# Tails of weight blocks gathered in DRAM, the second MLP weight loaded a group ahead, and two gelus moved at the seam

## The chip, the cores and the metric

The kernel runs on one core of one Trainium2 chip. A core has TensorE (matmuls into PSUM), VectorE, ScalarE, GpSimd and SyncE; in the kernel's text they are `pe`, `dve`, `act`, `pool` and `sp`. DMAs are issued here from SyncE (plain copies) and from GpSimd (copies that add to what lies at the destination, `accum_op`). Each engine works through its own instructions in the order in which the program issues them. The metric is the device time of one execution in microseconds, lower is better.

## The reference

The input x has 2048 tokens of 576 channels, all in float32. With xn = layernorm(x), the output is x plus an attention block on xn plus a mixer block on xn.

```python
# A: attention, 32 heads of 18, a window of 8 keys at distances 0, 2, ... 14
qkv = xn @ wqkv;  attn = softmax(q . k[s - off] / sqrt(18))
A = (attn @ v) @ wo
# B: shift mixing, then an MLP with 4608 hidden channels
h  = gelu(layernorm(xn) @ w1);  hs = four quarters of h, shifted by +1, -1, +2, -2 tokens
x1 = xn + hs @ w2
B  = x1 + gelu(layernorm(x1) @ w3) @ w4
out = x + A + B
```

The change lies in the MLP, w3 (576 x 4608) and w4 (4608 x 576), which takes over half of the time.

## The kernel before

Each float32 operand is split into a high part (type fp32r, made by ScalarE with a cast) and a low remainder (made by VectorE with a subtract), and a product is built of high-high, high-low and low-high matmuls. The low part of a 64-row tail shares a tile with its high part.

The program runs in stages: the projection to q, k, v; the token mixing (`mix_tile`, `mix_rem`, loop over four blocks b of 512 tokens and five column tiles i); x1; and then the MLP. The hidden channels of the MLP are worked off in chunks of 256. The first four chunks (`NPL = 4`) are plain. The remaining 14 (`NWP`) are done twice, once for each half of the tokens (sb = 0, 1): 28 groups q = 0 to 27. The second half goes through the chunks backwards (`pair(q)`), so that groups 13 and 14, the seam, share their weights.

In a group, a 2 x 2 block product (two halves of the 576 rows of w3, two hidden tiles of 128, two token blocks) is made from seven products instead of eight, from sums of blocks: of the weights (`combine`, VectorE, four instructions at line 956) and of the activations (DRAM sums `td`, GpSimd's accumulating DMAs in `sums`). `product` (line 1117) issues seven matmuls for each product, in the order of `HALVES`; the last of them, (0, 0), reads the tail rows of the weight. The seven products are called P1 to P7; they are interleaved with eight down tiles, D0 to D7, which multiply the gelus of the group before with w4 (`down`, matmuls at line 862). D0 to D3 read the hidden tiles c12 and c22, D4 to D7 read c11 and c21. c12, c21 and c22 have one buffer each. A down tile is accumulated in one of two PSUM buffers, which ScalarE (lines 867, 870) or VectorE (873) evicts; `ahead` then opens the buffer for the tile after next, for some tiles with a copy of the sum so far (843).

The order of the work around this is written out by hand. `ORDER` gives the sequence of a usual group, and `plan` holds, for each item, what is issued behind it:

```python
ORDER = "P1 D0 P2 P6 D1 P5 D2 P7 D3 P4 D4 P3 D5 D6 D7"
ORDERS = {..., NWP - 1: "P1 D0 P2 P6 P5 P7 D1 P4 P3 D2 D3 D4 D5 D6 D7",
          NWP: "D0 D1 P1 D2 P2 P6 D3 P5 P7 D4 P4 P3 D5 D6 D7"}
```

The steps of a group, as far as the change touches them:

- `load_pair(q)` (lines 945 and 948, SyncE) loads the chunk's part of w3 into the one staging tile `w3st` (`WS["st", q]`): two DMAs of 256 KB and four of 64 KB, the tail rows once for each 32 partitions. It is issued for a later group at D6, when `w3st` is free.
- `split_a(n)` makes the tile `w3a` of the next group from three plain blocks of `w3st`: step 0 a cast on ScalarE (961), step 1 a signed copy of the tail rows on ScalarE (963) and an accumulating DMA from GpSimd (964) that adds the raw tail rows onto 32 partitions, so that these hold the remainder, step 2 a subtract on VectorE (967). Steps 0 and 1 are issued at D1, step 2 at D2.
- `combine(n)` overwrites the blocks in `w3st` with their sums. It is issued at P4.
- `split_s(n)` makes `w3s`, which has one buffer, from the sums in the same three steps (at P3 and D5); its accumulating DMA reads the sums in `w3st`.
- `load_w4(c)` (560, SyncE) loads 576 KB of w4 into unused parts of Y, at P1 of its own group; `split_w4(c)` casts it on ScalarE (567, at D3) and subtracts on VectorE (570, at D4).
- `gelu22` and `gelu12` (814, 815, ScalarE) write c22 and c12, `low22` and `low12` (820, VectorE) their low parts; `z_add` is line 1127, `keep` line 1123.
- At the seam, `get_op` (911, 913) loads the activations of the second half of the tokens, and `split_op` (921, 926, 927 on ScalarE, 595 on VectorE) splits them, in two parts each: B11, B21, T2, T1, T3, T4, B22.
- Attention runs in the gaps: `bg` lets a generator issue so many microseconds of VectorE work behind each item, with its loads and stores on SyncE (693, 696, 722), until a few groups before the end. In the last groups `load_o` (1165), `o_turn` and `put_o` prepare its output, and a last stage multiplies that with wo.

Of the kernel before, what the change touches and what calls it, by code (L numbers as in the profile page):

```python
# [8 lines left out]
F32 = mybir.dt.float32  # L9
F32R = mybir.dt.float32r  # L10
AF = mybir.ActivationFunctionType
ALU = mybir.AluOpType
# [4 lines left out]
S, D, F = 2048, 576, 4608  # L17
# [12 lines left out]
HF = D // 2  # L30
# [27 lines left out]
def fused_block(ctx, tc, x, wqkv, wo, w1, w2, w3, w4, out):  # L58
# [36 lines left out]
    xd = {}  # L95
    qkvd = dram.tile([24, HALO + S, GC], F32, name="qkvd")
    od = dram.tile([S, D], F32, name="od")
    yd = {t: dram.tile([128, D], F32, name=f"yd{t}") for t in YD}
    xn = [dram.tile([D, 512], F32, name=f"xn{b}") for b in range(NB)]
    td = {(sb, k): dram.tile([HF, 512], F32, name=f"td{sb}{k}")  # L100
# [405 lines left out]
    for b in range(NB):  # L506
        for i, m in enumerate((0, 1, 2, 4, 3) if b < 3 else (4, 0, 1, 2, 3)):
            if m < 4:
                mix_tile(b, m)
            else:  # L510
                todo += mix_rem(b)
            if b + 1 < NB and i in (1, 2):
                split_x(xring["z", b + 1], i - 1)
            for _ in range((0, 1, 1, (1, 2, 2, 2, 3)[i])[b]):
                todo.pop(0)()
            if b == 0 and i < 2:
                w2raw[i] = load_w2(i)
            if b + 2 < NB and i == 4:
                get(("z", b + 2), ring_block(("z", b + 2)))
            k = {(0, 4): 0, (1, 1): 1, (1, 4): 2, (2, 1): 3, (2, 4): 4}.get((b, i))  # L520
            if k is not None:
                split_w(W2[:, k, :], W2[:, 5 + k, :], w2raw[k])
                if k < 3:
                    w2raw[k + 2] = load_w2(k + 2)
# [27 lines left out]
        spent[0] += 0.82  # L552
        split_w(W3[f][:, 0:5, :], W3[f][:, 5:10, :], raws[f])

    def load_w4(c, eng=sp):
        t = W4["pair", c] = wp.tile([128, 2, 2, D], F32R, name="w4", bufs=2)
        for i in range(2):
            f = 2 * c + i
            W4[f] = t[:, i]
        eng.dma_start(Y[:, 0:4, :].rearrange("p (a b) c -> p a b c", b=2)[:, :, 1, :],  # L560
                      w4[c * 256:(c + 1) * 256, :].rearrange("(a p) d -> p a d", p=128))

    def split_w4(c, step=None):
        t = W4["pair", c]
# [372 lines left out]
    def pair(q):  # L937
        return q if q < NWP else 2 * NWP - 1 - q
# [17 lines left out]
            dve.tensor_tensor(st[:, :, o, :], st[:, :, o, :], st[:, :, i, :], op=op)  # L956


    def split_ws(dst, src, steps):
        if 0 in steps:  # L960
            act.copy(dst[:, 3:5], src[:, 1:3])  # L961
        if 1 in steps:
            act.activation(dst[0:96, 0], src[0:96, 0], AF.Identity, scale=TS)
            pool.dma_start(dst[32:64, 0].bitcast(F32), src[32:64, 0], accum_op=ALU.add)
        if 2 in steps:
            spent[0] += 1.1
            dve.tensor_tensor(dst[:, 1:3], src[:, 1:3], dst[:, 3:5].bitcast(F32), op=ALU.subtract)

    def split_a(q, steps=(0, 1, 2)):
        if 0 in steps:  # L970
            WA[q] = wp.tile([128, 15, 128], F32R, name="w3a", bufs=2).rearrange(
                "p (s o) c -> p s o c", s=5)
        split_ws(WA[q], WS["st", q][:, :, 1:4, :], steps)

    def split_s(q, steps=(0, 1, 2)):
        if 0 in steps:
            WS[q] = wspool.tile([128, 20, 128], F32R, name="w3s").rearrange(
                "p (s o) c -> p s o c", s=5)
        split_ws(WS[q], WS["st", q], steps)

    def place(k):
        return opool.tile([128, 5, 512], F32R, name=f"big{k}")
# [199 lines left out]
    for q in range(NQ):  # L1182
# [33 lines left out]
        def at(it, f, *args):  # L1216
            plan.setdefault(it, []).append(lambda: f(*args))
# [13 lines left out]
            at("P3", load_pair, q + 2)  # L1231
        elif q == NWP - 1:
            rtemps[:] = [2, 13]
            at("P1", load_w4, p)
            for it, k in zip(("P1", "P2", "P6", "P5", "P7", "P4", "P3"),
                             ("B11", "B21", "T2", "T1", "T3", "T4", "B22")):
                at(it, get_op, 1, k)
            at("P4", split_w4, p)
            at("P4", gelu22)
            at("P3", split_op, 1, "B11", 0)  # L1240
            at("P3", low22)
            at("D2", split_op, 1, "B11", 1)
            at("D2", gelu12)
            at("D3", split_op, 1, "B21", 0)
            at("D4", low12)
            at("D4", split_op, 1, "B21", 1)
            at("D5", split_op, 1, "T2", 0)
            at("D6", split_op, 1, "T2", 1)
            at("D7", split_op, 1, "T1", 0)
        elif q == NWP:  # L1250
            rtemps[:] = [2]
            at("D0", split_op, 1, "T1", 1)
            at("D1", split_op, 1, "T3", 0)
            at("P1", split_op, 1, "T3", 1)
            at("D2", split_op, 1, "T4", 0)
            at("P2", split_a, n, (0, 1))
            at("P6", split_a, n, (2,))
            at("P6", split_op, 1, "T4", 1)
# [8 lines left out]
            at("D5", split_s, n, (2,))  # L1267
            at("D6", low12)
        elif z < -1:
            at("P1", load_w4, p)  # L1270
            at("D1", split_a, n, (0, 1))
            at("D2", split_a, n, (2,))
            at("D3", split_w4, p, 0)
            at("P4", combine, n)
            at("P4", gelu22)
            at("D4", low22)
            at("D4", split_w4, p, 1)
            at("P3", split_s, n, (0, 1))
            at("D5", gelu12)
            at("D5", split_s, n, (2,))  # L1280
# [11 lines left out]
        if -5 <= z <= -2:  # L1292
            for i, (it, nx) in enumerate((("P6", "D1"), ("P7", "D3"), ("P3", "D5"), ("D6", "D7"))):
                t = 4 * (z + 5) + i
                at(it, o_turn, t)
                if t + 3 < NT:
                    at(nx, load_o, t + 3)

        if 0 < q < 9:
            at("D6", sums, 1, q - 1)  # L1300
        if 0 < q <= len(YD):
# [1 line left out]
        if -4 <= z < -1:  # L1303
            at("P1", put_o, z + 4)
        if z == -2:
            at("D7", load_w4, NPL + pair(q + 1))
            at("D7", put_o, 3)

        if z == -1:
# [147 lines left out]
```

## Time and profile before

| | |
|---|---|
| median of 3 runs | 1311.72 us (1311.17 to 1312.82) |
| the profiled execution | 1307.43 us |
| its span, first to last instruction | 1305.7 us |
| mean granted clock of TensorE | 0.990 |
| busy: TensorE matmuls, weight loads | 1263.4 us, 1158.4 us |
| busy: VectorE, ScalarE, GpSimd | 919.9, 747.8, 258.9 us |
| moved by DMA | 226.14 MB, 173 GB/s in the mean |

PE is TensorE's matmuls and PEld its weight loads, which run beside them; DVE is VectorE, ACT ScalarE, POOL GpSimd, SPq SyncE's queue of DMA issues. A row of the timeline gives the start and the duration in microseconds, the engine and line, the operation, the tiles written and read with their shapes, how many instructions were merged, and in brackets how long the engine had been idle before it and what ended that. A wait for several things is put down to the one that came last by the profile. A row of the groups gives the busy time, the mean duration in ns of one, and the idle time before them. In a row of the chain of waits there are start, duration and what ran. The last numbers of a row of a window are the granted clock, the DMA engines' busy share and GB/s; before them stand the window's length and the busy time of PE, PEld, DVE, ACT and POOL. A row of DMA issues ends with the KB of one and the median time from issue to landing in microseconds.

### The profile page before, as it was taken

To read this page: it belongs to the slowest core of one execution; us is meant where nothing else is said; L and a number is where in the kernel's file an instruction comes from. 1 tells how busy PE (TensorE), PEld (TensorE's weight loads), DVE (VectorE), ACT (ScalarE), POOL (GpSimd) and SP (SyncE) were. 2 spreads that over 40 slices of the span, in tenths; PEclk is the share of its full clock that TensorE was granted. 3 is DMA by queue.
4 is the path that set the end of the run, shared out by engine and by line. 5 is a ranking of instruction groups with operands and counts; after the bars stand their busy time and mean duration, and the time that the engine had idled before them with its cause. 6 is when DMAs were issued, how large, how long until landed. Compare 5 with 4: busy or idle time off the path is not lost.

```text
span 1305.7 us, 20016 instructions
## 1 busy us (share of the span) xinstructions
PE 1263.4 (97%) x7482; PEld 1158.4 (89%) x7482; DVE 919.9 (70%) x1226; ACT 747.8 (57%) x1188; POOL 258.9 (20%) x374
## 2 busy tenths in 40 slices
PE   9999999999999999899979999989999999999998
PEld 8999998899889998788968889978999989998898
DVE  6456535778468987579967989978999994455342
ACT  4322226536546546677656677757777767667730
POOL 2011100021221121123222232212222222222100
PEclk9999999999999999999989999989999999999999
DMA  7646874256888898479878779795876767899982
GB/s 212 154 109 149 171 159 145 69 159 181 192 214 202 194 217 193 88 180 202 192 166 169 193 135 214 165 230 123 206 163 111 184 124 147 194 217 221 252 252 82
DMA packets 204641, 226.14 MB, mean 173 GB/s; under 512 B 79856, under 2 KB 139728, under 8 KB 204416
## 3 DMA queue, kind: packets, MB, share of 16 engines
q1 hardware_dynamic: 171408, 157.60, 42.0%
q0 software_dynamic: 33136, 67.26, 31.9%
q8 instruction: 59, 0.97, 0.3%
q14 instruction: 38, 0.31, 0.1%
HBM read 125.76 MB, written 107.28 MB: 178 GB/s over the span
## 4 chain that ended last, share of the span: by engine, by line
PE 29%; issue 6%; DMA 5%; DVE 5%; ACT 3%; SPq 1%; POOL 1%; DVEq 0%; POOLq 0%; ACTq 0%
PE ps L862 13%; PE cc L1117 11%; PE ps L214 4%; DVE w3st L956 1%; DMA w3st<-in_B_w_dram 1%; DMA w3a<-w3st 1%; DVE po L716 1%; DMA Y<-in_B_w_dram 1%; POOL yd L868 1%; DMA x1n<-xd 1%; DMA yd<-ev 1%; DVE po L720 1%; DVE c L820 0%; DMA yd<-Y 0%; ACT Y L867 0%
## 5 line engine op out<-in xcount | busy, mean ns | idle before, releaser
L862 PEld LDWEIGHTS ps<-w,c 128*128 128x128 f32 x3456 | 483.5, 190 | 48.3 <-ACT Y L867 18.6
L862 PE MATMUL ps<-w,c 128*128 128x288 f32 x3456 | 497.9, 297 | 28.2 <-ACT Y L867 15.9
L868 POOL DMA_DIRECT2D yd<-Y x154 | 140.1, 913 | 389.7 <-ACT Y L867 325.9
L820 DVE TENSOR_TENSOR c<-Y,c 128x512 fp32r<-128x512 f32 x144 | 98.8, 687 | 80.3 <-ACT Y L809 71.9
L1117 PE MATMUL cc<-xt,w3s 128*128 128x512 f32 (+1 forms) x588 | 150.2, 395 | 5.2 <-DVE Y L1127 5.2
L867 ACT COPY Y<-ps 128x576 f32<-128x576 f32 x154 | 97.4, 633 | 71.0 <-PE ps L862 65.0
L214 PE MATMUL ps<-WQ,xt 128*128 128x432 f32 x672 | 134.8, 360 | 0.0
L1117 PEld LDWEIGHTS cc<-xt,w3s 128*128 128x128 f32 (+1 forms) x588 | 108.0, 189 | 26.7 <-DVE Y L1127 5.9
L214 PEld LDWEIGHTS ps<-WQ,xt 128*128 128x128 f32 x672 | 125.6, 188 | 5.7
L1117 PE MATMUL cc<-x1n,w3a 128*128 128x512 f32 x392 | 102.9, 402 | 1.9 <-DMA w3a<-w3st 0.8
L740 DVE TENSOR_TENSOR po<-q,k 128x1152 f32<-128x1152 f32 (+1 forms) x48 | 84.2, 1754 | 6.1 <-DMA od<-po 5.3
L1117 PEld LDWEIGHTS cc<-x1n,w3a 128*128 128x128 f32 x392 | 72.6, 193 | 15.9 <-ACT Y L815 1.2
L743 DVE TENSOR_REDUCE L<-po 128x64 f32<-128x1152 f32 (+1 forms) x48 | 84.0, 1751 | 0.9
L121 POOL TENSOR_TENSOR rs<-rs,mhalf 128x1 f32<-128x1 f32 x48 | 30.9, 643 | 258.1 <-DVE rs L120 147.7
L956 DVE TENSOR_TENSOR w3st<-w3st 128x384 f32<-128x384 f32 x108 | 60.2, 557 | 28.6 <-DMA w3a<-w3st 15.6
L323 ACT COPY stg<-ps 128x864 f32<-128x864 f32 x24 | 21.1, 881 | 102.7 <-PE ps L214 55.8
L870 ACT COPY Y<-ps 128x576 f32<-128x576 f32 x92 | 58.8, 639 | 33.7 <-PE ps L862 31.9
L716 DVE TENSOR_TENSOR po<-v,L 128x1152 f32<-128x1152 f32 x56 | 75.5, 1353 | 0.9
L720 DVE TENSOR_TENSOR po<-po 128x1152 f32<-128x1152 f32 x49 | 66.4, 1355 | 1.0
L843 ACT COPY ps<-Y 128x576 f32<-128x576 f32 x92 | 59.3, 645 | 3.9 <-DVE Y L873 1.5
L1127 DVE TENSOR_TENSOR Y<-cc,Y 128x512 f32<-128x512 f32 x57 | 39.1, 685 | 26.1 <-ACT Y L1123 24.9
L961 ACT CAST w3s<-w3st 128x1024 fp32r<-128x1024 f32 x27 | 28.4, 1050 | 46.2 <-DVE w3st L956 31.6
(190 smaller groups left out, 1921.9 us busy)
## 6 DMA issues: line engine op xcount, KB each, us to landing
yd<-Y POOLq DMA_DIRECT2D x156, 288.0 KB, 5.7
Y<-in_B_w_dram SPq DMA_DIRECT2D x31, 576.0 KB, 7.2
w3st<-in_B_w_dram SPq DMA_DIRECT2D x60, 256.0 KB, 6.5
qkvd<-stg SPq DMA_DIRECT2D x24, 432.0 KB, 3.5
yd<-ev POOLq DMA_DIRECT2D x26, 288.0 KB, 6.7
w3st<-in_B_w_dram SPq DMA_DIRECT2D x108, 64.0 KB, 6.7
xd<-st SPq DMA_DIRECT2D x16, 320.0 KB, 6.1
xd<-big SPq DMA_DIRECT2D x16, 320.0 KB, 7.9
```

The costliest lines, as they stand in the source:

```text
L214: pe.matmul(ps[:, h, :n], xs(a), ws(b, h), start=i == 0, stop=i == len(PAIRS) - 1)
L716: dve.tensor_tensor(dst, vv, Lf[:, :, w:w + 1].to_broadcast([128, TPP * GH, HD]), op=ALU.mult)
L720: dve.tensor_tensor(o, o, dst, op=ALU.add)
L740: dve.tensor_tensor(dst, qf[:, None, :].to_broadcast([128, n, TPP * GC]), win, op=ALU.mult)
L743: dve.tensor_reduce(Lw[:, w:w + n, :], dst.rearrange("p w (x d) -> p w x d", d=HD), axis=AX.X, op=ALU.add)
L820: dve.tensor_tensor(h[:, 1, :], g, h[:, 0, :].bitcast(F32), op=ALU.subtract)
L843: act.copy(ps[:, :, :HF], halves(t))
L862: pe.matmul(ps[:, k, :HF], h[:, col], w[:, p, k * HF:(k + 1) * HF], start=n == 0 and not seed, stop=n == len(seq) - 1, skip_group_check=True)
L867: act.copy(e.rearrange("p (h c) -> p h c", h=2), ps[:, :, :HF])
L868: pool.dma_start(yd[t], e, accum_op=ALU.add)
L956: dve.tensor_tensor(st[:, :, o, :], st[:, :, o, :], st[:, :, i, :], op=op)
L1117: pe.matmul(ps, WX[w][:k, v, SLOT[w], :], area[sb][xk][:k, a, :], start=onto is None and i == 0, stop=last and i == len(HALVES) - 1, skip_ ...
```

## The change

There are three parts. First, the tail rows of the three plain blocks of each chunk are gathered once, during token mixing (b = 1, i = 2 and 3), by two DMAs from w3 into a DRAM tile `w3t` (14 x 32 x 384 floats), and the accumulating DMA of `split_a` reads them from there instead of from `w3st`; `combine` moves from P4 to D3. Second, the load of w4 is parted from the allocation of its split tile and is issued a group earlier, at D5 (in group 0 at P3); in the usual groups `split_w4` moves from D3 and D4 to D4 and D5. Third, in group 13 gelu22 moves from P4 to D3, low22 from P3 to D4, gelu12 from D2 to D5 and low12 from D4 to D6, and the splits of the activations in groups 13 and 14 move one to two items later.

```diff
@@ -95,6 +95,7 @@
     xd = {}
     qkvd = dram.tile([24, HALO + S, GC], F32, name="qkvd")
     od = dram.tile([S, D], F32, name="od")
+    w3t = dram.tile([NWP, 32, 384], F32, name="w3t")
     yd = {t: dram.tile([128, D], F32, name=f"yd{t}") for t in YD}
     xn = [dram.tile([D, 512], F32, name=f"xn{b}") for b in range(NB)]
     td = {(sb, k): dram.tile([HF, 512], F32, name=f"td{sb}{k}")
@@ -515,6 +516,10 @@
                 todo.pop(0)()
             if b == 0 and i < 2:
                 w2raw[i] = load_w2(i)
+            if b == 1 and i in (2, 3):
+                r0, c0, n = ((256, 128, 128), (HF + 256, 0, 256))[i - 2]
+                sp.dma_start(w3t[:, :, 128 * (i - 2):128 * (i - 2) + n],
+                             dram_ap(w3, r0 * F + 256 * NPL + c0, [[256, NWP], [F, 32], [1, n]]))
             if b + 2 < NB and i == 4:
                 get(("z", b + 2), ring_block(("z", b + 2)))
             k = {(0, 4): 0, (1, 1): 1, (1, 4): 2, (2, 1): 3, (2, 4): 4}.get((b, i))
@@ -552,13 +557,14 @@
         spent[0] += 0.82
         split_w(W3[f][:, 0:5, :], W3[f][:, 5:10, :], raws[f])
 
-    def load_w4(c, eng=sp):
-        t = W4["pair", c] = wp.tile([128, 2, 2, D], F32R, name="w4", bufs=2)
-        for i in range(2):
-            f = 2 * c + i
-            W4[f] = t[:, i]
-        eng.dma_start(Y[:, 0:4, :].rearrange("p (a b) c -> p a b c", b=2)[:, :, 1, :],
-                      w4[c * 256:(c + 1) * 256, :].rearrange("(a p) d -> p a d", p=128))
+    def load_w4(c, part=None):
+        if part != 0:
+            t = W4["pair", c] = wp.tile([128, 2, 2, D], F32R, name="w4", bufs=2)
+            for i in range(2):
+                W4[2 * c + i] = t[:, i]
+        if part != 1:
+            sp.dma_start(Y[:, 0:4, :].rearrange("p (a b) c -> p a b c", b=2)[:, :, 1, :],
+                         w4[c * 256:(c + 1) * 256, :].rearrange("(a p) d -> p a d", p=128))
 
     def split_w4(c, step=None):
         t = W4["pair", c]
@@ -956,12 +962,12 @@
             dve.tensor_tensor(st[:, :, o, :], st[:, :, o, :], st[:, :, i, :], op=op)
 
 
-    def split_ws(dst, src, steps):
+    def split_ws(dst, src, steps, tails):
         if 0 in steps:
             act.copy(dst[:, 3:5], src[:, 1:3])
         if 1 in steps:
             act.activation(dst[0:96, 0], src[0:96, 0], AF.Identity, scale=TS)
-            pool.dma_start(dst[32:64, 0].bitcast(F32), src[32:64, 0], accum_op=ALU.add)
+            tails(dst[32:64, 0].bitcast(F32))
         if 2 in steps:
             spent[0] += 1.1
             dve.tensor_tensor(dst[:, 1:3], src[:, 1:3], dst[:, 3:5].bitcast(F32), op=ALU.subtract)
@@ -970,13 +976,17 @@
         if 0 in steps:
             WA[q] = wp.tile([128, 15, 128], F32R, name="w3a", bufs=2).rearrange(
                 "p (s o) c -> p s o c", s=5)
-        split_ws(WA[q], WS["st", q][:, :, 1:4, :], steps)
+        split_ws(WA[q], WS["st", q][:, :, 1:4, :], steps,
+                 lambda t: pool.dma_start(t, w3t[pair(q)].rearrange("p (o c) -> p o c", o=3),
+                                          accum_op=ALU.add))
 
     def split_s(q, steps=(0, 1, 2)):
         if 0 in steps:
             WS[q] = wspool.tile([128, 20, 128], F32R, name="w3s").rearrange(
                 "p (s o) c -> p s o c", s=5)
-        split_ws(WS[q], WS["st", q], steps)
+        st = WS["st", q]
+        split_ws(WS[q], st, steps,
+                 lambda t: pool.dma_start(t, st[32:64, 0], accum_op=ALU.add))
 
     def place(k):
         return opool.tile([128, 5, 512], F32R, name=f"big{k}")
@@ -1231,28 +1241,28 @@
             at("P3", load_pair, q + 2)
         elif q == NWP - 1:
             rtemps[:] = [2, 13]
-            at("P1", load_w4, p)
+            at("P1", load_w4, p, 1)
             for it, k in zip(("P1", "P2", "P6", "P5", "P7", "P4", "P3"),
                              ("B11", "B21", "T2", "T1", "T3", "T4", "B22")):
                 at(it, get_op, 1, k)
             at("P4", split_w4, p)
-            at("P4", gelu22)
             at("P3", split_op, 1, "B11", 0)
-            at("P3", low22)
             at("D2", split_op, 1, "B11", 1)
-            at("D2", gelu12)
-            at("D3", split_op, 1, "B21", 0)
-            at("D4", low12)
-            at("D4", split_op, 1, "B21", 1)
-            at("D5", split_op, 1, "T2", 0)
-            at("D6", split_op, 1, "T2", 1)
-            at("D7", split_op, 1, "T1", 0)
+            at("D3", gelu22)
+            at("D4", low22)
+            at("D4", split_op, 1, "B21", 0)
+            at("D5", gelu12)
+            at("D5", split_op, 1, "B21", 1)
+            at("D6", low12)
+            at("D6", split_op, 1, "T2", 0)
+            at("D7", split_op, 1, "T2", 1)
         elif q == NWP:
             rtemps[:] = [2]
-            at("D0", split_op, 1, "T1", 1)
-            at("D1", split_op, 1, "T3", 0)
-            at("P1", split_op, 1, "T3", 1)
-            at("D2", split_op, 1, "T4", 0)
+            at("D0", split_op, 1, "T1", 0)
+            at("D1", split_op, 1, "T1", 1)
+            at("P1", split_op, 1, "T3", 0)
+            at("D2", split_op, 1, "T3", 1)
+            at("P2", split_op, 1, "T4", 0)
             at("P2", split_a, n, (0, 1))
             at("P6", split_a, n, (2,))
             at("P6", split_op, 1, "T4", 1)
@@ -1267,14 +1277,14 @@
             at("D5", split_s, n, (2,))
             at("D6", low12)
         elif z < -1:
-            at("P1", load_w4, p)
+            at("P1", load_w4, p, 1)
             at("D1", split_a, n, (0, 1))
             at("D2", split_a, n, (2,))
-            at("D3", split_w4, p, 0)
-            at("P4", combine, n)
+            at("D3", combine, n)
             at("P4", gelu22)
+            at("D4", split_w4, p, 0)
             at("D4", low22)
-            at("D4", split_w4, p, 1)
+            at("D5", split_w4, p, 1)
             at("P3", split_s, n, (0, 1))
             at("D5", gelu12)
             at("D5", split_s, n, (2,))
@@ -1296,6 +1306,8 @@
                 if t + 3 < NT:
                     at(nx, load_o, t + 3)
 
+        if z < -1 and q + 1 != NWP:
+            at("D5" if q else "P3", load_w4, NPL + pair(q + 1), 0)
         if 0 < q < 9:
             at("D6", sums, 1, q - 1)
         if 0 < q <= len(YD):
@@ -1303,7 +1315,7 @@
         if -4 <= z < -1:
             at("P1", put_o, z + 4)
         if z == -2:
-            at("D7", load_w4, NPL + pair(q + 1))
+            at("D7", load_w4, NPL + pair(q + 1), 1)
             at("D7", put_o, 3)
 
         if z == -1:
```

## The prediction

> **What bounds the kernel now.** I read the page first, then the chain that ended last, then the timeline of TensorE's weight loads over the paired stage (about 512 to 1243 us), and last the timeline of all engines around each hole found there.
>
> ```profile
> span 1305.7 us, 20016 instructions
> PE 1263.4 (97%) x7482; PEld 1158.4 (89%) x7482; DVE 919.9 (70%) x1226; ACT 747.8 (57%) x1188; POOL 258.9 (20%) x374
> L956 DVE TENSOR_TENSOR w3st<-w3st 128x384 f32<-128x384 f32 x108 | 60.2, 557 | 28.6 <-DMA w3a<-w3st 15.6
> ```
>
> TensorE is the bound: 97% of the span. Only its holes can be won, since the change alters no matmul. The third line is `combine`: VectorE stood idle 28.6 us ahead of it, 15.6 of that for the accumulating DMA into `w3a`, which reads the very tile that `combine` overwrites.
>
> A group without a hole is seen in the chain, product to product:
>
> ```profile
> 912.31 1.62 PE cc L1117 x7
> ...
> 936.43 1.61 PE cc L1117 x7
> ```
>
> That is 24.12 us (seven products of 1.62 and eight down tiles of 1.59 make 24.06). The holes of the other groups, from the weight loads; in brackets the idle time and who ended it:
>
> ```profile
> 538.89 1.60 PEld L862 LDWEIGHTS ps<-w,c 128*128 128x128 f32 x8 [2.27 <-DVE c L820]
> 586.73 1.61 PEld L862 LDWEIGHTS ps<-w,c 128*128 128x128 f32 x12 [1.82 <-ACT Y L867]
> 612.48 1.61 PEld L862 LDWEIGHTS ps<-w,c 128*128 128x128 f32 x12 [1.66 <-ACT Y L867]
> 670.18 2.90 PEld L862 LDWEIGHTS ps<-w,c 128*128 128x128 f32 x12 [9.17 <-ACT Y L867]
> 719.43 1.97 PEld L1117 LDWEIGHTS cc<-xt,w3s 128*128 128x128 f32 x7 [3.34 <-DVE Y L1127]
> 725.54 1.63 PEld L862 LDWEIGHTS ps<-w,c 128*128 128x128 f32 x12 [1.32 <-ACT Y L870]
> 778.11 2.79 PEld L862 LDWEIGHTS ps<-w,c 128*128 128x128 f32 x12 [2.27 <-ACT Y L867]
> 876.31 11.51 PEld L862 LDWEIGHTS ps<-w,c 128*128 128x128 f32 x72 [5.15 <-issue]
> 1055.94 1.62 PEld L862 LDWEIGHTS ps<-w,c 128*128 128x128 f32 x12 [1.04 <-ACT Y L867]
> ```
>
> The largest one, followed back:
>
> ```profile
> 660.04 1.14 POOL L964 DMA_DIRECT2D w3a<-w3st  x1
> 665.52 2.33 DVE L956 TENSOR_TENSOR w3st<-w3st 128x384 f32<-128x384 f32 x4 [8.65 <-DMA w3a<-w3st]
> 667.94 1.05 ACT L961 CAST w3s<-w3st 128x1024 fp32r<-128x1024 f32 x1 [10.81 <-DVE w3st L956]
> 669.51 0.62 ACT L867 COPY Y<-ps 128x576 f32<-128x576 f32 x1
> ```
>
> GpSimd issues the small accumulating DMA late, VectorE holds `combine` back until it has landed, ScalarE stands 10.81 us at the split of `combine`'s result, and the eviction behind it on ScalarE is what TensorE needs for D7.
>
> **The change part by part.** After such a hole the matmuls are slow for a while:
>
> ```profile
> 670.18 3.25 PE ps L862 x12
> 673.43 2.80 PE cc L1117 x7
> ...
> 778.11 3.14 PE ps L862 x12
> 781.25 1.87 PE cc L1117 x7
> ```
>
> D7 and P1 took 6.05 us after the hole of 9.17 and 5.01 after that of 2.27, where 1.59 + 1.62 = 3.21 is usual: 2.84 and 1.80 us on top. After the hole of 1.82 (586.73) twelve loads took the usual 1.61, so there is nothing on top. The Trainium skill ("TensorE: Matmul & The Clock Gate", Part 1) says the clock halves after an idle window of about 3.4 us; by that rule the 2.27 hole would give back only itself, and the sum would be 1.8 less. The row shows the slow matmuls, so I go by the row.
>
> ```profile
> 638.50 1.48 PEld L1117 LDWEIGHTS cc<-x1n,w3a 128*128 128x128 f32 x7
> 535.85 0.47 PE L1117 MATMUL cc<-x1n,w3a 96*128 96x512 f32 x1 [0.78 <-DMA w3a<-w3st]
> 535.89 2.34 DVE L956 TENSOR_TENSOR w3st<-w3st 128x384 f32<-128x384 f32 x4 [1.69 <-ACT Y L815]
> w3a<-w3st POOLq DMA_DIRECT2D x27, 48.0 KB, 5.3
> w3s<-w3st POOLq DMA_DIRECT2D x27, 64.0 KB, 2.5
> yd<-in_A_x_dram POOLq DMA_DIRECT2D x10, 288.0 KB, 7.8
> ```
>
> *Tails from DRAM, `combine` at D3 instead of P4.* `combine` no longer waits for the DMA's read, only for the splits at D1 and D2, and it stands ahead of one slice of attention work on VectorE instead of behind it. Its result is read by ScalarE's split of `w3s` at P3. The three short holes 586.73, 612.48 and 1055.94 each have `combine` just before them: 1.82 + 1.66 + 1.04 = 4.5; I take 4.3. The hole 778.11 is of the same make: 2.27 + 1.80 = 4.1; I take 4.0. The hole 670.18 is 9.17 + 2.84 = 12.0. There the late DMA still has to land before the last matmul of the next P1 reads it. Without the hole, P1 begins at 638.50 + 24.12 = 662.6 and its seventh matmul some 1.4 later (its loads took 1.48), at 664.0. The DMA issued at 660.04 was there by 665.52, which would leave 1.5; but GpSimd's queue should run earlier, because W4's 576 KB no longer go out just before. I leave 1.0 and take 11.0.
>
> In group 1 the page blames ScalarE for `combine`'s wait, but TensorE's seventh matmul was let go by that DMA at the same moment, 535.85: it is the same landing. `combine` can go 1.69 earlier, and with it the low half that TensorE waits for at 538.89: of 2.27 I take 1.6.
>
> An accumulate that reads DRAM isn't in this trace at this size. Its ends are the 2.5 us of the `w3s` tails and the 7.8 of a DRAM accumulate six times as large; I take the 5.3 of the `w3a` tails, the same bytes to the same place. With the usual place at D1 there are over 10 us to the next P1 (the split at 921.81, further down, against 936.43), so only 670.18 feels the difference.
>
> *W4 a group ahead.* What it can win is one place:
>
> ```profile
> 711.44 0.84 SPq L560 DMA_DIRECT2D Y<-in_B_w_dram  x1
> 714.75 2.56 DVE L740 TENSOR_TENSOR po<-q,k 128x2304 f32<-128x2304 f32 x1 [5.30 <-DMA od<-po]
> 722.62 1.15 ACT L567 CAST w<-Y 128x1152 fp32r<-128x1152 f32 x1 [8.82 <-DMA Y<-in_B_w_dram]
> ```
>
> SyncE came to W4 7 us late behind attention's loads, and ScalarE waited 8.82. The hole at 725.54 goes: 1.3. The hole at 719.43 stays: VectorE's own 5.30 us for attention's store comes first. W4's copy moves from D3 to D4 on ScalarE and its subtract from D4 to D5 on VectorE. ScalarE's next work there, the `w3s` split, must wait for P3 to finish reading `w3s` anyway, so the copy sits in idle time; the subtract goes behind P3's `z_add`, which serves gelu12 sooner. Its new wait is SyncE's: the next W4 load stands at D5 until the subtract is done, with the load of the next W3 pair (D6) behind it. That load waits longer in any case, for the `w3s` accumulate:
>
> ```profile
> 912.85 0.98 SPq L945 DMA_DIRECT2D w3st<-in_B_w_dram  x2
> 921.81 0.62 ACT L963 ACTIVATE w3a<-w3st,kv 96x384 fp32r<-96x384 f32 x1
> 932.77 1.35 DVE L570 TENSOR_TENSOR w<-Y,w 128x1152 fp32r<-128x1152 f32 x1
> 912.00:936.00 24.00, 24.00 (x146) 21.84 (x145) 22.90 (x25) 16.64 (x28) 5.95 (x7) 1.00 0.82 195
> 1164.56 0.84 ACT L961 CAST w3a<-w3st 128x768 fp32r<-128x768 f32 x1 [1.34 <-DMA w3st<-in_B_w_dram]
> ```
>
> The next pair load is due near 912.85 + 24.1 = 936.9; the subtract ended at 934.1, so W4 gets a lead of about 2.8 us, and its 576 KB need 3.0 us at the window's 195 GB/s. The pair would be late by 0.2 us. In the last groups before the output stage SyncE is busy with attention's rows, the lead may be one or two microseconds shorter, and ScalarE already waits for the pair (1164.56). TensorE lost nothing from that 1.34. I charge 2.5 us over all groups, between 0 and the rival below.
>
> *The gather.* Two DMAs, 688 KB together, are added to SyncE's queue in the token-mixing stage, ahead of the third block's load. Two issues cost SyncE about 1 us (0.98 for two at 912.85); TensorE never idles there:
>
> ```profile
> L466 PE MATMUL ps<-xt,W 128*128 128x512 f32 x224 | 51.6, 389 | 0.0
> ```
>
> I take 0. Without that cover it would cost 688 KB at that 195 GB/s, 3.6 us, if the block's load had no slack.
>
> *The seam.* gelu22 of the last group of the first half stood at P4, ahead of D2 and D3 which still read the buffer it writes:
>
> ```profile
> 871.43 0.63 ACT L814 ACTIVATE c<-Y 128x512 fp32r<-128x512 f32 x1 [4.71 <-PE ps L862]
> ```
>
> ScalarE is held 4.71 us, VectorE behind it, so D2's eviction is late and D4 waits 5.15 us. The 72 loads after it took 11.51 where 6 x 1.61 = 9.66: 1.85 more. Behind D3 that wait is gone. Late next: D2's eviction behind the B11 split on VectorE, and the low half of gelu12, now only at D6, before the next D0. All splits from B21 to T4 move one to two slots later; TensorE wants T1 only at P5. Of 7.0 I leave 2.0 and take 5.0.
>
> Sum: 1.6 + 4.3 + 4.0 + 11.0 + 1.3 + 5.0 = 27.2, less 2.5, makes 24.7. The profiled execution took 1307.43 us, 1.7 more than its span, and lies 4.29 below the median 1311.72. 1307.4 - 24.7 = 1282.7; at the median 1287.0.
>
> **The rivals.** *The wait moves to TensorE.* If GpSimd stays as late as at 660.04 and the DRAM accumulate takes 7.8, it lands at 667.8, 3.8 after need, with some 1.8 of slow matmuls: 5.6 of the 12.0 stay instead of 1.0. If in addition all 7.0 of the seam stay, because VectorE is too full there, 24.7 - 4.6 - 5.0 = 15 is left: 1297. For it: the hole of 535.85 is just this wait. Against: the 14 us between 922.4 and 936.4 in a group without a hole.
>
> *Slower: W4 stands ahead of the pair.* If the lead comes to nothing, the pair lands 3.0 us later in each of 26 groups. 1.3 of that is free (1164.56); 1.7 x 26 = 44 us of holes against 27 won: 17 slower, 1329; it turns slower from a delay of 1.3 + 27/26 = 2.3 us on. For it: the split of the pair's tails at 921.81 runs 9 us after the load was issued, with hardly any room left in the late groups. Against: the lead of 2.8. The Trainium skill ("DMA: Bandwidth & Descriptors", Queues, rings and completion order) says that each engine takes descriptors in ring order, which is this rival's mechanism; an estimate from that page's fit, 590 KB at 436 GB/s, is 1.35 us, too little for it to turn.
>
> *More than forecast.* If SyncE's queue without W4 lets attention's store land sooner, the hole 719.43 (3.34 and its slow matmuls, about 5) goes too, and the leftovers 1.0, 2.0 and 2.5: 1287 - 10.5 = 1276.5 or a little lower.
>
> *Nothing*: each hole comes back at the next wait on the same engine, 1311.7.
>
> **How the numbers follow.** Forecast 0.62 (its own range 1278 to 1295), wait moves 0.16, more 0.08, nothing 0.04, slower 0.10. The range 1274 to 1303 takes in the first two and most of the third. About 0.2% is what a measurement of this kernel can tell from no change. Faster 0.62 + 0.16 + 0.08 = 0.86, same 0.04, slower 0.10.
>
> **What would show it.** Right: no DMA of `w3a` among `combine`'s releasers; ScalarE's wait before the `w3s` split falls from 10.81 to about 1 at most; no wait of L567 for W4; products 24.1 us apart from group 2 to 12 save the one with attention's store; gelu22 at the seam without a wait for D3. Wrong: ScalarE's splits of `w3a` waiting 2 us or more for the pair in most groups (slower), or TensorE's last matmul of P1 released by the accumulate (the first rival).

## The result and the profile after

The changed kernel takes 1297.12 us (median of 4 runs, 1295.08 to 1297.93) against 1312.27 for the kernel before (4 runs, 1311.17 to 1314.64): a ratio of 0.988 with the interval 0.9861 to 0.9898. Forecast were 24.7 us, and 1287.0; the runs give 15.2. The profiled execution of the changed kernel took 1295.08, against 1307.43 before: 12.4.

The page of the changed kernel:

```profile
span 1293.2 us, 20054 instructions
PE 1258.8 (97%) x7482; PEld 1150.9 (89%) x7482; DVE 916.6 (71%) x1226; ACT 746.0 (58%) x1188; POOL 259.4 (20%) x374
L962 DVE TENSOR_TENSOR w3st<-w3st 128x384 f32<-128x384 f32 x108 | 59.9, 555 | 2.8
w3st<-in_B_w_dram SPq DMA_DIRECT2D x60, 256.0 KB, 8.1
```

Its DMA issues, with KB each and the median us from issue to landing:

```profile
w3s<-w3st POOLq DMA_DIRECT2D x27, 64.0 KB, 2.5
w3a<-w3t POOLq DMA_DIRECT2D x27, 48.0 KB, 4.6
```

TensorE still holds 97% of the span. `combine` (now L962) had 28.6 us of idle time ahead of it, 15.6 of them for the accumulating DMA; now it has 2.8, and no DMA among its releasers. The accumulate that reads DRAM lands in 4.6 us, the one that read SBUF took 5.3; in the other kernels below that read DRAM it takes 4.6 to 5.7, and 5.6 where only the source was changed, so the source does not make it faster. One figure got worse: the loads of the W3 pairs (`w3st`) land in 8.1 us; before, they took 6.5.

How long the paired stage takes is seen from the first product's weights of its first and last group. Weight loads in the timeline, first the kernel before, then the changed one:

```profile
514.05 3.10 PEld L1117 LDWEIGHTS cc<-x1n,w3a 128*128 128x128 f32 x14
...
1203.02 1.48 PEld L1117 LDWEIGHTS cc<-x1n,w3a 128*128 128x128 f32 x7
```

```profile
517.09 3.10 PEld L1127 LDWEIGHTS cc<-x1n,w3a 128*128 128x128 f32 x14
...
1190.76 1.48 PEld L1127 LDWEIGHTS cc<-x1n,w3a 128*128 128x128 f32 x7
```

From 688.97 to 673.67: the stage gained 15.3 us. But it begins 3.0 later, at 517.09 instead of 514.05. 15.3 - 3.0 = 12.3, which is the 12.5 of the two spans but for 0.2 in the output stage. So there are two questions: why the stage gained 15 and not 25, and what costs 3 us ahead of it.

**The holes that went.** The holes of 586.73, 612.48, 670.18, 778.11 and 1055.94 are gone from their places. Taken from product to product, less the clean 24.06, the groups in question lost 11.75 (hole 670.18 and the group behind it), 3.8 (778.11) and 4.6 (the three short ones) before. The first two groups together took 48.3 before and 45.5 after, 2.8 less. That makes 23 us. Just behind the place of the largest hole the changed kernel has a smaller one that is new. Eviction and then weight load there:

```profile
664.29 0.64 ACT L873 COPY Y<-ps 128x576 f32<-128x576 f32 x1 [1.91 <-DMA yd<-Y]
...
665.47 1.46 PEld L1127 LDWEIGHTS cc<-x1n,w3a 128*128 128x128 f32 x7 [1.30 <-ACT cc L1330]
```

ScalarE waits 1.91 us for one of GpSimd's accumulates (`yd`) before it can evict, and the copy behind that eviction is what P2 waits for. This group is 1.4 us over the clean time.

**A wait that is new.** ScalarE's waits for the W3 pair before the split of `w3a`, in us, times and longest, before and after:

```profile
ACT w3a L961 <- DMA w3st<-in_B_w_dram: 4.0, 3, 2.0
```

```profile
ACT w3a L967 <- DMA w3st<-in_B_w_dram: 35.9, 19, 4.0
```

In 19 groups the pair is now late. The timeline of the changed kernel around group 4 shows what becomes of it:

```profile
608.84 0.79 POOL L989 DMA_DIRECT2D w3s<-w3st  x1 [4.93 <-ACT w3s L969]
...
610.27 0.38 SPq L566 DMA_DIRECT2D Y<-in_B_w_dram  x1
...
615.46 0.94 SPq L951 DMA_DIRECT2D w3st<-in_B_w_dram  x2
...
624.17 0.83 ACT L967 CAST w3a<-w3st 128x768 fp32r<-128x768 f32 x1 [3.87 <-DMA w3st<-in_B_w_dram]
624.91 0.61 ACT L969 ACTIVATE w3a<-w3st,kv 96x384 fp32r<-96x384 f32 x1
...
626.66 0.58 ACT L1133 COPY Y<-cc 128x512 f32<-128x512 f32 x1
...
627.29 1.45 PEld L1127 LDWEIGHTS cc<-xt,w3a 128*128 128x128 f32 x7 [1.48 <-ACT Y L1133]
```

SyncE issues W4's load first, then the pair's. ScalarE waits 3.87 us for the pair; the copy of a product's result out of PSUM (L1133) stands behind the two split instructions on ScalarE, and TensorE needs that copy before P4. That makes a hole of 1.48. Such holes ahead of P4 stand at seven places outside the seam, of 0.5, 1.5, 1.6, 0.5, 1.6, 0.7 and 1.6: about 8 us. The kernel before had a single one, of 0.63, in group 14, inside the seam.

**Ahead of the stage.** The gather is issued just ahead of a block's load (L174) in the token-mixing stage. Before, then after:

```profile
228.60 1.06 SPq L173 DMA_DIRECT2D xt<-xd  x2
...
233.50 0.62 ACT L180 CAST xt<-xt 64x512 fp32r<-64x512 f32 x1 [0.46 <-DMA xt<-xd]
...
240.60 0.30 PEld L481 LDWEIGHTS ps<-xt,W1R 128*128 128x128 f32 x2 [0.23 <-DVE xt L187]
```

```profile
223.64 0.99 SPq L521 DMA_DIRECT2D w3t<-in_B_w_dram  x1
...
229.76 0.88 SPq L521 DMA_DIRECT2D w3t<-in_B_w_dram  x1
230.74 1.78 SPq L174 DMA_DIRECT2D xt<-xd  x2
...
236.24 0.62 ACT L181 CAST xt<-xt 64x512 fp32r<-64x512 f32 x1 [1.88 <-DMA xt<-xd]
...
240.05 0.30 PEld L482 LDWEIGHTS ps<-xt,W1R 128*128 128x128 f32 x2 [1.14 <-ACT g L473]
240.99 0.99 PEld L482 LDWEIGHTS ps<-xt,W1R 128*128 128x128 f32 x5 [0.64 <-ACT xt L187]
...
243.34 0.30 PEld L482 LDWEIGHTS ps<-xt,W1R 128*128 128x128 f32 x2 [1.37 <-DVE xt L188]
```

The split of the block's first rows (L180, L181) comes 2.7 us later. By these rows that is the time SyncE spends on issuing, not the time of the bytes: the two gather issues take it 0.99 and 0.88 us, so it reaches the block's load 2.1 us later, and the load's own two issues take 1.78 instead of 1.06. From the end of those issues to the split it is 3.8 us before and 3.7 after. The split chain behind it is late, and TensorE, which had a hole of 0.23 there, has three, 3.2 together.

**At the seam** the hole of 5.15 is gone: 72 loads run without a break. Weight loads of the changed kernel:

```profile
854.96 9.79 PEld L868 LDWEIGHTS ps<-w,c 128*128 128x128 f32 x72
865.56 1.62 PEld L868 LDWEIGHTS ps<-w,c 128*128 128x128 f32 x12 [0.82 <-ACT Y L873]
869.14 1.62 PEld L868 LDWEIGHTS ps<-w,c 128*128 128x128 f32 x12 [1.96 <-ACT Y L873]
...
882.44 1.45 PEld L1127 LDWEIGHTS cc<-x1n,w3s 128*128 128x128 f32 x7 [1.21 <-ACT Y L1133]
...
887.00 1.44 PEld L1127 LDWEIGHTS cc<-xt,w3a 128*128 128x128 f32 x7 [1.31 <-ACT Y L1133]
```

In its place come holes for evictions (L873) and copies (L1133) that stand on ScalarE behind the splits which were moved back by one or two slots. The eviction of 869.14, for instance, stands at 868.47 behind this split:

```profile
867.51 1.06 ACT L927 ACTIVATE xt<-xt 128x1024 fp32r<-128x1024 f32 x1 [2.00 <-DMA xt<-td1T]
```

The two groups of the seam were 10.46 us over the clean time before (7.08 and 3.38), and are 9.06 now.

### The profile page after: what moved, and what is told of

It reads as the page before. It is cut to its first block, busy times and chain, and to the rows that moved or that the text cites. A ratio compares the mean times of both kernels' runs of the same rounds, so it can differ in the third digit from the quotient of the medians.

```text
span 1293.2 us, 20054 instructions
## 1 busy us (share of the span) xinstructions
PE 1258.8 (97%) x7482; PEld 1150.9 (89%) x7482; DVE 916.6 (71%) x1226; ACT 746.0 (58%) x1188; POOL 259.4 (20%) x374
## 4 chain that ended last, share of the span: by engine, by line
PE 29%; DMA 9%; DVE 4%; ACT 4%; issue 3%; SPq 1%; POOL 0%; DVEq 0%; ACTq 0%; POOLq 0%
PE ps L868 13%; PE cc L1127 11%; DMA w3st<-in_B_w_dram 5%; PE ps L215 4%; DMA xt<-td1T 1%; DMA od<-po 1%; DVE w3st L962 1%; DMA x1n<-xd 1%; DMA Y<-od 1%; DMA yd<-Y 1%; ACT Y L873 0%; DVE c L826 0%; DVE Y L1137 0%; DVE po L722 0%; ACT Y L876 0%
## 5 line engine op out<-in xcount | busy, mean ns | idle before, releaser
L868 PEld LDWEIGHTS ps<-w,c 128*128 128x128 f32 x3456 | 477.2, 188 | 28.7 <-ACT Y L873 4.8
L868 PE MATMUL ps<-w,c 128*128 128x288 f32 x3456 | 490.9, 295 | 9.1 <-ACT Y L873 3.2
L873 ACT COPY Y<-ps 128x576 f32<-128x576 f32 x154 | 97.8, 636 | 67.3 <-PE ps L868 55.9
L962 DVE TENSOR_TENSOR w3st<-w3st 128x384 f32<-128x384 f32 x108 | 59.9, 555 | 2.8
L1127 PE MATMUL cc<-xt,w3a 128*128 128x512 f32 (+1 forms) x196 | 50.8, 398 | 7.3 <-ACT Y L1133 7.3
```

The lines of the kernel that those rows point to most:

```text
L868: pe.matmul(ps[:, k, :HF], h[:, col], w[:, p, k * HF:(k + 1) * HF], start=n == 0 and not seed, stop=n == len(seq) - 1, skip_group_check=True)
L873: act.copy(e.rearrange("p (h c) -> p h c", h=2), ps[:, :, :HF])
L1127: pe.matmul(ps, WX[w][:k, v, SLOT[w], :], area[sb][xk][:k, a, :], start=onto is None and i == 0, stop=last and i == len(HALVES) - 1, skip_ ...
```

## The experiments

The theory after these readings: the tails in DRAM bring the gain, as forecast or a little more; W4's rows ahead of the pair cost 6 to 8 us and win nothing; the gather costs about 3 at the place where it stands; the seam is worth about half of what was forecast. The rival for the first: it is the earlier place of `combine`, not the tails' source. The rival for the second: the pair is late for some other reason than W4, such as more traffic. The kernel before was run in each set on the same chip, with medians of 1313.08, 1315.36 and 1316.18 in the three sets, so kernels of different sets are compared by their ratios.

**W4's rows behind the pair.** In the planner of the paired stage:

```
-            at("D5" if q else "P3", load_w4, NPL + pair(q + 1), 0)
+            at("D6" if q else "P3", load_w4, NPL + pair(q + 1), 0)
```

> The changed kernel with one line different: W4's load for the next group is issued at D6 behind the load of the W3 pair instead of at D5 ahead of it. Theory 1, the order in SyncE's queue: ScalarE's wait for the pair before the split of w3a (35.9 us in 19 places in the changed kernel) falls back to about the 4 us of before, the holes ahead of P4 (577, 627, 806, 831, 1107, 1156, 1181 us, together about 8) go, and the time is 6 to 8 us below the 1297.1 of the changed kernel, about 1290. Theory 2, the pair is late because the groups follow each other faster and the DMA engines are full: ScalarE's wait stays above 25 us and the time within 2 us of 1297.

Measured: 1291.07 us (1289.84 to 1291.8), ratio 0.9826 (0.9795 to 0.9856). ScalarE's waits:

```profile
ACT w3a L967 <- DMA w3st<-in_B_w_dram: 10.1, 7, 2.7
```

35.9 us fell to 10.1 (not quite to the 4 that were expected), and of the seven holes ahead of P4 one is left, of 0.36. The page's row of the pair's landing:

```profile
w3st<-in_B_w_dram SPq DMA_DIRECT2D x60, 256.0 KB, 6.2
```

So order in SyncE's queue is the cause: behind W4 the 256 KB loads land in 8.1 us (median), ahead of it in 6.2. The Trainium skill's rule, cited in the prediction ("DMA: Bandwidth & Descriptors", Queues, rings and completion order), agrees; the estimate of 1.35 us from that page's fit for the delay was too low beside the 1.9 measured. The order costs in a second way, which this run undoes at the same time: SyncE can't issue W4 before W4's subtract has ended, and the pair stands behind it. In the group with the hole of 806.47 the subtract ends at 790.71, W4 goes out at 790.73 and the pair at 791.91, 4.07 us behind the issue of the `w3s` accumulate, where 2.7 is usual in the kernel before. How the 8 us divide between the two ways is not shown. In group 4 a third effect is seen, DMA issues from 605 to 620 us with their median time to landing, first the changed kernel, then this one:

```profile
w3s<-w3st POOLq DMA_DIRECT2D x1, 64.0 KB, 6.5
```

```profile
w3s<-w3st POOLq DMA_DIRECT2D x1, 64.0 KB, 3.6
```

The pair's load waits for GpSimd's accumulate of the `w3s` tails, and there that accumulate took 6.5 us beside W4's transfer. This is not the rule: over all groups its median is 2.5 in both kernels. In the group after, W4 was issued 0.8 us behind the accumulate and the pair went out as usual, 2.7 us behind it. So why it was slow here stays open.

**The gather two blocks later.**

```
-            if b == 1 and i in (2, 3):
+            if b == 3 and i in (2, 3):
```

> The changed kernel with the two gathering DMAs moved from the second block of the token mixing (b = 1) to the last (b = 3), where no block is loaded behind them. If they delay the third block's load, as the trace of the changed kernel suggests (mixing ends at 256.2 instead of 253.4 us), TensorE's three waits at 240 to 243 us go and 2.7 us come back: about 1294.4. If the loss comes from the DMA engines' work as such, it appears again at b = 3 or stays: 1297.

Measured: 1291.93 us (1290.87 to 1296.71), ratio 0.984 (0.9805 to 0.9875). Its weight loads at the place in question:

```profile
239.29 1.55 PEld L482 LDWEIGHTS ps<-xt,W1R 128*128 128x128 f32 x7
241.13 0.30 PEld L482 LDWEIGHTS ps<-xt,W1R 128*128 128x128 f32 x2 [0.29 <-DVE xt L188]
```

The three holes are back to one of 0.29, SyncE issues the block's load at 229.06 in 1.06 us, and the split comes at 234.03, so they were the gather's. What this is worth in time is not shown as well: the intervals of the ratios overlap. By the profile the gain is lost again before the paired stage, which begins at 517.94 here (517.09 in the changed kernel, 514.05 before), and at 514.86 to 516.89 in the four later runs with the same gather. A hole at 501.73, where TensorE waits for an eviction by VectorE, is 2.64 long here, 1.6 to 2.5 in the later runs, and 1.30 in the changed kernel. It doesn't need the gather: in the run of `combine` alone below, which has no gather and no change ahead of that place, it is 2.30 against 1.02 before. The profiled run was also this kernel's longest. In all three pairs of kernels that differ by the gather's place the ratio is lower with the later one, by 0.003 to 0.004, but in each pair the intervals overlap.

**W4 in its own group again**, with its loads and splits where the kernel before had them; all else as changed:

```
-            at("P1", load_w4, p, 1)
+            at("P1", load_w4, p)
...
+            at("D3", split_w4, p, 0)
...
-            at("D4", split_w4, p, 0)
...
-            at("D5", split_w4, p, 1)
+            at("D4", split_w4, p, 1)
...
-            at("D5" if q else "P3", load_w4, NPL + pair(q + 1), 0)
...
```

> The changed kernel without its second part: W4 is loaded at P1 of its own group and split at D3 and D4 as before; the tails still come from DRAM, combine stays at D3, the seam stays changed. Theory 1: the holes ahead of P4 go (about 8 us), the D0 hole behind the late subtract at 716 to 719 us (2.3) goes, and the wait of ScalarE for W4 near 722 us comes back with about 1.8 us of holes: 1288 to 1290, faster than the changed kernel, so that this part of the change costs time. Theory 2 (traffic): 1297 to 1299.

Measured: 1290.36 us (1286.83 to 1295.82), ratio 0.9825 (0.9783 to 0.9866). ScalarE's waits:

```profile
ACT w L573 <- DMA Y<-in_B_w_dram: 26.9, 4, 16.2
```

The wait for W4 in the stage is back (26.9 in four; the longest, about 16, is in every kernel here), of the holes ahead of P4 one of 0.17 is left, and the time is that of W4 behind the pair.

**The seam as before.** The seam's lines of the diff undone: gelu22 at P4, the splits B21 to T4 in their old slots.

> The changed kernel with the plan of groups 13 and 14 as before (gelu22 at P4, gelu12 at D2, the splits one to two items earlier); W4 ahead and the tails from DRAM stay. The forecast put 5.0 us on this part: 1302. The two traces instead show groups 13 and 14 together 10.5 us over 48.1 before and 9.1 over it after: 1298.5, which this run tells apart.

Measured: 1300.84 us (6 runs, 1297.27 to 1305.16), ratio 0.9906 (0.9874 to 0.9938). Its weight loads:

```profile
862.04 9.50 PEld L868 LDWEIGHTS ps<-w,c 128*128 128x128 f32 x60 [5.16 <-issue]
...
887.40 1.45 PEld L1127 LDWEIGHTS cc<-xt,w3a 128*128 128x128 f32 x7 [0.84 <-ACT Y L1133]
```

The hole of 5.16 is back, the two holes for evictions (0.82, 1.96) are gone, and of the two for copies (1.21, 1.31) one of 0.84 is left. The two groups of the seam are 12.0 us over the clean time here and 9.06 with the change: 3 us by the profiles. The ratio's interval overlaps that of the changed kernel, so the times alone don't show it.

**Both mended**: W4 behind the pair and the gather two blocks later, together.

> The changed kernel with both mends at once: W4's load at D6 behind the load of the W3 pair, and the gather in the last block of the token mixing. If the two losses are separate, their gains add: 1297.1 less 6 for the order in SyncE's queue, less 2.7 to 5 for the gather, 1286 to 1289, ratio to before about 0.979. If the second mend only shifts the same wait, 1290 to 1291, as with W4 behind the pair alone.

Measured: 1289.12 us (1288.26 to 1289.46), ratio 0.98 (0.9779 to 0.982), clear of the changed kernel's interval, but not of that of W4 behind the pair alone (0.9795 to 0.9856). So the runs don't tell whether the two gains add.

**The tails alone**: the kernel before, with the tails gathered in DRAM and accumulated from there (the first part of the diff), `combine` at P4, W4 and the seam as before.

> The kernel before with the tails of the plain blocks gathered in DRAM (in the second mixing block, as in the change) and accumulated from there; combine stays at P4, W4 and the seam stay as before. Theory: combine's wait for the accumulating DMA (15.6 us) goes and with it most of the holes at 670 and 778 us (16.1 with their slow matmuls); part of 586 and 612 stays, since combine also stands behind a slice of attention; the gather costs 2.7. About 12 us below before, 1300. Rival: combine's place at P4 makes it late anyway, and less than 6 us are won.

Measured: 1298.65 us (1293.45 to 1300.59), ratio 0.9869 (0.9832 to 0.9905), with the gather still at its costly place: as much as the whole change (0.988). The row of `combine` on its page:

```profile
L961 DVE TENSOR_TENSOR w3st<-w3st 128x384 f32<-128x384 f32 x108 | 59.9, 555 | 2.8
```

**`combine` alone**: the kernel before, with one line changed:

```
-            at("P4", combine, n)
+            at("D3", combine, n)
```

> The kernel before with combine issued at D3 instead of P4 and nothing else; the tails still come from the staging tile, so combine still waits for the accumulating DMA. Theory: the holes in which that DMA is late (670, 778 us) stay or grow, since VectorE now stands at combine from D3 on; only the hole at 1056 us and parts of 586 and 612 go: 0 to 3 us below before, 1310 to 1313. Rival: the place of combine is what matters; then 5 us or more are won.

Measured: 1318.77 us (10 runs, 1316.13 to 1324.28), ratio 1.0029 (1.0012 to 1.0046): a little slower, where 0 to 3 us less were expected. Its timeline around the large hole:

```profile
667.87 1.14 POOL L964 DMA_DIRECT2D w3a<-w3st  x1
...
673.35 2.33 DVE L956 TENSOR_TENSOR w3st<-w3st 128x384 f32<-128x384 f32 x4 [10.48 <-issue]
```

`combine` stands earlier in VectorE's order and waits all the same. The profile names no releaser here ("issue"), but `combine` starts 5.5 us after the small DMA was issued at 667.87, just as before (660.04 to 665.52), where the profile names that DMA. What is new is that more work is queued behind it: VectorE stands idle ahead of `combine` for 46.0 us in all, where it was 28.6. So the rival falls: the gain is that the DMA no longer reads that tile. Whether the earlier place is worth something once the tails lie in DRAM was not tried by itself. The tails alone still have five holes of 0.3 to 1.0 us ahead of D7, 2.8 together, at 587.47, 612.08, 660.90, 686.79 and 1046.95, and the changed kernel has none there; that suggests a few microseconds.

**W4's worth and place, once mended.** In one set: both mended once more; W4 in its own group with the gather two blocks later; and both mended with W4's copy and subtract one slot earlier:

```
-            at("D4", split_w4, p, 0)
+            at("D3", split_w4, p, 0)
...
-            at("D5", split_w4, p, 1)
+            at("D4", split_w4, p, 1)
```

> The kernel with both parts mended once more, on the same chip as the two beside it, so that differences of one or two us can be read: 1289, ratio to the kernel before 0.980 to 0.983.

> The changed kernel with the gather two blocks later and with W4's rows loaded in their own group again, as in the kernel before: of the change there remain the DRAM tails with the earlier combine, and the seam. If W4's lead is worth anything once it stands behind the pair, this is slower than the kernel with both parts mended: by the W4 hole of 1.3 and its successor, 1 to 4 us. If the lead is worth nothing (theory: the hole was covered by attention's late store anyway), the two agree within 2 us, about 1290.

> The kernel with both parts mended (W4 behind the pair, gather two blocks later), and W4's copy and subtract back at D3 and D4 instead of D4 and D5. If the wait of D0 for W4's subtract (0.90, then 1.44 for the low half behind it) comes from the later place, it goes and 1 to 3 us are won: 1286 to 1288. If VectorE's late attention step sets it anyway, the same within 1 us: 1289.

Measured: both mended again 1288.96 us (1286.44 to 1291.5), ratio 0.9793 (0.9754 to 0.9833). W4 in its own group 1286.44 (1284.67 to 1291.39), ratio 0.9787 (0.9748 to 0.9825). Earlier split 1286.96 (1285.43 to 1288.92), ratio 0.9785 (0.9752 to 0.9819). The three can't be told apart: W4 a group ahead wins nothing even where it costs nothing. W4 in its own group needs the least code and has the lowest median, about 28 us under the kernel before by its ratio. As to the earlier split, D0's wait for W4's subtract (0.90) is gone, but it is gone from both mended again too, which has the later split, so this is not shown to be the earlier split's doing. The wait behind attention's store is long in both. Weight loads of both mended again, then of the earlier split:

```profile
706.53 2.63 PEld L1127 LDWEIGHTS cc<-xt,w3s 128*128 128x128 f32 x7 [5.11 <-DVE Y L1137]
```

```profile
708.18 2.63 PEld L1127 LDWEIGHTS cc<-xt,w3s 128*128 128x128 f32 x7 [5.49 <-DVE Y L1137]
```

The first of these is the same kernel as both mended, which had 3.66 there: at this place two executions of one kernel differ by more than the edit could bring.

## Why the prediction was right or wrong

The direction, the mechanism of the main part and the range were right; the size was 9.5 us too large by the medians, 12.3 by the two profiles. Point by point, in us of the profiles:

- **Tails and `combine`: right, a little more.** Forecast 1.6 + 4.3 + 4.0 + 11.0 = 20.9; measured 2.8 + 4.6 + 3.8 + 11.75 = 23.0, or 21.6 without the 1.4 of the new hole at 665.47. No DMA among `combine`'s releasers, as forecast, and `combine`'s place alone wins nothing. The accumulate from DRAM, taken at 5.3 between 2.5 and 7.8, took 4.6 here and 4.6 to 5.7 in the other runs. The 1.0 left at 670.18 was meant for its landing. In the changed kernel no wait for it is seen; the 1.30 of 665.47, just behind, has another cause, so that the size came out is luck. With W4 behind the pair the wait that was meant, the first rival's, does show up in that place as 1.60, with both mended as 1.1 to 1.9. One sign did not come true: from group 2 to 12 the products are not all 24.1 us apart. Besides the two groups at attention's store, five are 0.5 to 1.9 longer.
- **W4 a group ahead of the pair: 2.5 was charged, about 8 was paid.** The step that failed is the lead of 2.8 us. It was read from the end of W4's subtract in the trace of before, 934.1, with the subtract at D4, though the change itself puts it at D5. The timeline of the changed kernel in a group without holes:

```profile
944.00 1.35 DVE L576 TENSOR_TENSOR w<-Y,w 128x1152 fp32r<-128x1152 f32 x1
945.38 0.38 SPq L566 DMA_DIRECT2D Y<-in_B_w_dram  x1
...
945.99 1.79 PE L1127 MATMUL cc<-x1n,w3a 128*128 128x512 f32 x7
...
946.56 0.90 SPq L951 DMA_DIRECT2D w3st<-in_B_w_dram  x2
```

  Here the subtract ends, at 945.35, 0.6 us before the group's first product; in the kernel before it ended some 2.3 before it (934.1 against the chain's 936.43). W4 is issued 1.2 us ahead of the pair, not 2.8. With W4's 3.0 us the pair is then late by 1.8, and its landing did grow by 1.6. The prediction's own slower rival has the price: 1.3 of such a delay is free, so (1.6 - 1.3) x 26 = 7.8, and the holes came to 8. That the two agree so well is luck: the holes stand in seven groups, not 0.3 us in each of 26, and part of them comes from the pair's late issue. It did not turn slower since that needed 2.3. The rival was right in its mechanism, and its condition came true by halves.
- **The hole at W4: 1.3 was forecast, nothing came.** The wait for W4 went, but W4's subtract, moved to D5, stands behind attention's late step on VectorE and became the next wait of the following D0:

```profile
702.46 2.56 DVE L746 TENSOR_TENSOR po<-q,k 128x2304 f32<-128x2304 f32 x1 [5.01 <-DMA od<-po]
...
707.14 1.46 PEld L1127 LDWEIGHTS cc<-xt,w3s 128*128 128x128 f32 x7 [3.05 <-DVE Y L1137]
...
715.38 1.35 DVE L576 TENSOR_TENSOR w<-Y,w 128x1152 fp32r<-128x1152 f32 x1
...
716.78 0.30 PEld L868 LDWEIGHTS ps<-w,c 128*128 128x128 f32 x2 [0.90 <-DVE w L576]
...
718.52 1.09 PEld L868 LDWEIGHTS ps<-w,c 128*128 128x128 f32 x8 [1.44 <-DVE c L826]
```

  The two groups were 6.84 over the clean time before, and are 7.49. That attention's store (5.01 here, 5.30 before) keeps its hole was forecast.
- **The gather: 0 was taken, 2.7 was paid at its place**, and the stage begins 3.0 later, inside the bound of 3.6. But that bound was for the bytes, and what the rows show is the issuing: 1 us was taken for the two issues, and they took 0.99 + 0.88, with 0.7 more for the issues of the load behind them. The cover named was the row of L466, where TensorE never idles. But the block whose load stands behind the gather also has the products of L481, which read the split rows of that very load; the right row to ask was the wait of the split at 233.50 in the trace of before, 0.46 us: a load that is already waited for has no slack.
- **The seam: 5.0 was taken, the profiles give 1.4 against the kernel before and 3 against the same kernel with the old seam.** The wait of gelu22 went as forecast. The step that failed is the 2.0 left for what is late next: the splits one or two slots later stand ahead of evictions on ScalarE, and ScalarE now reaches two of these splits before their loads have landed (2.00 at 867.51, 1.12 at 871.52), so that evictions (0.82, 1.96) and copies (1.21, 1.31) took the place of most of the 5.15.

Added up: +0.7 for the tails (21.6 against 20.9), -5.5 for the pair (8 against 2.5), -2.0 for W4's hole, -2.8 for the gather and -3.6 for the seam make -13.2. Holes of 0.4 to 0.7 us in other groups, which nobody forecast, went and give back about 1.2. That makes -12.0 of the 12.3 that are missing between the profiles. The medians miss 2.8 less, since the profiled execution of before lies 4.8 below the median of its four runs and that of the changed kernel 2.0.

## What to carry to other kernels

Where a small DMA holds back the instruction that overwrites its source, take the source away rather than move the instruction: here that alone brought as much as the whole change, and moving alone lost a little. When a load is put ahead in a queue, find the load behind it, take the releasing instruction where the change puts it and not where the old trace has it, and go through the groups one by one: here the delay made holes in seven of 26, 8 us together, a third of the gain that was forecast. Count each DMA issue on its own engine too: two of nearly 1 us put off the load behind them. Whether a load has slack is asked of its own consumer's wait, not of a busy engine nearby.

## What was not expected of the hardware

- An accumulating DMA of 48 KB into SBUF took about as long from DRAM as from SBUF: a median of 5.3 us from SBUF in the kernel before, and 5.6 from DRAM where only the source was changed. It was 4.6 to 4.8 in the three kernels that issue W4 ahead of the pair and 5.2 to 5.7 in the others, so it goes with W4's place; how is not shown.
- A 64 KB accumulate on GpSimd's queue took 6.5 us instead of the usual 2.5 where a 576 KB load from SyncE's queue was issued 1.4 us behind it; with that load 7 us behind it, in the same group, it took 3.6. One group shows this, and in the next one such a load 0.8 us behind did no harm, so the cause is open.
- Two gathers from DRAM to DRAM (224 and 448 KB) took SyncE 0.99 and 0.88 us to issue, and the load behind them 1.78 instead of 1.06. The split that reads this load came 2.7 us later, which is the issuing time.
- Slow matmuls do not follow from the length of a hole alone. Seven weight loads took 1.46 us after the hole of 3.05 (707.14, changed kernel) and 2.63 after those of 5.11 and 5.49; but in the kernel before twelve took 2.79 after a hole of 2.27, where 1.61 is usual. The idle window of about 3.4 us that the Trainium skill gives ("TensorE: Matmul & The Clock Gate", Part 1) agrees with the first three and not with the fourth. Nor do two holes of one length agree with each other: seven weight loads took 1.45 us after 3.66 (706.48, both mended) and 2.63 after 3.64 (707.71, the gather two blocks later).
